# A retention layer and a top-1 mixture of experts in one launch: engine orders written by hand, compact states, and gathers that follow the scatters

## The chip, the core and the metric

The kernel runs on one core of one Trainium2 chip. The core has a matrix engine (PE; its weight loads are listed as PEld), a vector engine (DVE), a scalar engine (ACT), a general engine (POOL) and a queue engine (SP) that only starts transfers. PE reads from on-chip memory (SBUF) and writes to the accumulator memory (PSUM), which DVE and ACT empty. Transfers from and to HBM run on 16 DMA engines that all queues share. The metric is the device time of one execution in microseconds (us), as the median of several.

## The reference, cut to what matters

First a retention layer (decay gamma per head, state of 64x64 per head) over 4 batches, 8 heads and 768 positions; its output, 3072 rows of 512, goes into a mixture of experts with 8 experts, where a row is computed only if its skip score is positive, and then by the one expert with the largest logit.

```python
for t in range(S):                       # S = 768, D = 64, H = 8, B = 4
    state = gamma[None, :, None, None] * state + einsum('bhd,bhe->bhde', k[:, :, t], v[:, :, t])
    y[:, :, t] = scale * einsum('bhd,bhde->bhe', q[:, :, t], state)
x = y.transpose(0, 2, 1, 3).reshape(B * S, H * D)      # 3072 x 512
do_compute = (x @ w_skip) > 0
logits = x[do_compute] @ w_gate                          # 8 experts
e_idx = argmax(logits);  gate_w = softmax(logits)[e_idx]
out = x.copy()
out[rows of expert e] += gate_w * (relu(x @ w1[e]) @ w2[e])   # 512 -> 1024 -> 512
```

With the inputs of this case 1510 of the 3072 rows are computed; the experts get 191, 133, 229, 179, 211, 187, 160 and 220 of them.

## The kernel before, in words

**Stage 1, retention.** The recurrence is cut into 6 chunks of 128 positions per head, and two heads (a pair) are one unit: 4 batches x 4 pairs = 16 units. The decay is put into q and k beforehand (`scale_qk`, L85, on POOL: one instruction for k, one for q, in all units). A unit i then consists of these steps, most of them on PE in fp32, where a matmul becomes two instructions and a transpose one:

- `t_qk` (L198): 12 transposes of 128x128 in four groups of three; ACT copies each group from PSUM (L206) into KT and QT.
- `s_at` (L208), in two halves: k times q inside a chunk, as 64x64 tile matmuls (64 rows, 64 columns of the array), 24 instructions a half. DVE multiplies the two PSUM tiles of a half with the causal mask (L224) into ATm.
- `s_kv` (L230): 40 instructions of 64x64 tiles for k times v; DVE adds them up to running states Zb (L250, L252), in 10 instructions, one per chunk and head, each 64x64. Zb holds the two heads' states as blocks on the diagonal of a 128x128 tile whose other blocks are zero (L131 to L134).
- `s_inter` (L254), for unit i-1: 10 instructions, state times q, with the whole 128x128 array.
- `s_av` (L264), for unit i-1: 48 instructions of 64x64 tiles, ATm times v, into the same PSUM tiles Y; ACT copies them to xT (L276).
- `t_x` (L280), for unit i-2: 6 transposes back to rows; ACT copies them (L288) into xall, and after a batch's last pair xall is stored to the output tensor (L293).

After each batch come the gate's steps: `gate_logits` (L299), `gate_rows` (L311: logits, maximum, one-hot choice, softmax, running places per expert), and `slot_table` (L374), which gathers for every expert a table of up to 256 row numbers and gate weights by matmuls with one-hot matrices.

**Stage 2, experts.** `slots` (L435) makes row indices `si` from the table; empty slots get an index out of bounds, whose rows a transfer skips. `gather` (L453) fetches an expert's 256 rows from the output tensor with two indirect transfers on POOL. Then for each expert: `x_tr` (L462: DVE cast, 4+4 transposes, DVE copies), `layer1` (L474: 32 matmuls, relu on ACT), `layer2` (L490: 2 x 16 matmuls; DVE scales and adds, L499, into one of four buffers yo; POOL scatters, L502). PE's order is x_tr(e+1) ahead of layer2(e). The scatters are declared independent of each other, since their rows are distinct; gathers and scatters are not, so they are ordered on the output tensor.

**What sets the order.** A planner orders the instructions of PE, DVE, ACT and SP from priorities and its own estimates; POOL's order is as written (L69) up to the end of the gathers (L516). On POOL all 16 gathers (L513) and the late weight loads (L515) are written ahead of the first scatter. Expert weights (1 MB as bf16 each, 16 of them, cast on the way from fp32) are loaded by POOL's queue: eight are issued in stage 1 (`wunits`, L393), one right after it, seven between the gathers. q, k and v come by SP's queue, three units ahead (L398), 384 KB each.

Of the kernel before, what the change touches and what calls it, by code (L numbers as in the profile page):

```python
# [9 lines left out]
FP32 = mybir.dt.float32  # L10
# [8 lines left out]
def kernel(  # L19
# [36 lines left out]
    NEARLY = 5  # L56
    BIG = 1.0e6
# [10 lines left out]
    stP = ExitStack()  # L68
    stP.enter_context(tc.manual_schedule(engines={mybir.EngineType.Pool}))  # L69
# [15 lines left out]
    def scale_qk(i):  # L85
# [5 lines left out]
        for w, t, tag in ((kw, tk, "ks"), (qw, tq, "qs")):  # L91
# [3 lines left out]
            G_.tensor_tensor(o[:, :, :, :], in_, sc, ALU.mult)  # L95
            w[i] = o

    load(0)

# [11 lines left out]
    A_.activation(out=tq[:, :, :], in_=nlg[:, :, :], func=AF.Exp, bias=0.0, scale=1.0)  # L111
    V_.tensor_scalar(tq[:, :, :], tq[:, :, :], scale, None, ALU.mult)  # L112

    ident = poolC.tile([128, 128], FP32, name="ident")
    make_identity(nc, ident[:, :])

    load(1)
    scale_qk(0)


    maskc = poolC.tile([128, 4, R, 64], FP32, name="maskc")
    for r in range(R):
        for rq in range(R):
            for hi in range(2):
                V_.memset(maskc[64 * hi : 64 * hi + 64, r, rq, :], 1.0)
                G_.affine_select(
                    out=maskc[64 * hi : 64 * hi + 64, r, rq, :], in_=maskc[64 * hi : 64 * hi + 64, r, rq, :],
                    pattern=[[R, 64]], base=rq - r, channel_multiplier=-R, compare_op=ALU.is_ge, fill=0.0,
                )
    V_.tensor_copy(maskc[:, R : 2 * R, :, :], maskc[:, 0:R, :, :])  # L130
    Zb = [[poolC.tile([128, 128], FP32, name=f"Zb{s}_{c}") for c in range(1, NCH)] for s in range(2)]  # L131
    for zs in Zb:
        for z in zs:
            V_.memset(z[:, :], 0.0)  # L134
    load(2)

    identb = poolC.tile([128, 128], BF16, name="identb")
    V_.tensor_copy(identb[:, :], ident[:, :])
    ut_f = poolC.tile([128, 128], FP32, name="ut_f")
    make_upper_triangular(nc, ut_f[:, :], val=1.0, diag=False)  # L140
    utb = poolC.tile([128, 128], BF16, name="utb")
    V_.tensor_copy(utb[:, :], ut_f[:, :])
    onesb = poolC.tile([128, 128], BF16, name="onesb")
    V_.memset(onesb[:, :], 1.0)
    iota_i = poolC.tile([128, CAP], I32, name="iota_i")
    G_.iota(iota_i[:, :], pattern=[[1, CAP]], base=0, channel_multiplier=0)
    iotab = poolC.tile([128, CAP], BF16, name="iotab")
    V_.tensor_copy(iotab[:, :], iota_i[:, :])

# [434 lines left out]
```

## Time and profile before

| what | value |
|---|---|
| median of 3 runs | 260.09 us (256.2 to 260.12) |
| the profiled execution's own time | 257.54 us |
| its span, first to last instruction | 255.6 us |
| mean granted PE clock | 0.932 |
| PE busy | 204.7 us (80%) |
| DVE / ACT / POOL busy | 122.4 / 83.8 / 96.2 us |
| moved by DMA | 48.68 MB, mean 190 GB/s |

A busy PE is not PE at its peak: matmuls overlap, and what counts is the time from the start of one group to the start of the next. In the timeline's rows the columns are start, duration, engine, line and operation, output<-input, shape, number of instructions, and in brackets the idle time before the group with what ended it. Rows of the windows view give the stretch, its length, busy time (and instructions) of PE, PEld, DVE, ACT and POOL, the granted PE clock, the DMA engines' mean share and GB/s.

### The profile page before, as it was taken

The numbers are of one execution on the slowest core, as the hardware profiler recorded it, in microseconds if no ns is written. First come the engines' busy times: TensorE is split into PE (matmuls) and PEld (weight loads), VectorE is DVE, ScalarE is ACT, GpSimd is POOL, SyncE is SP. The second block draws the span as 40 slices with busy tenths as digits, with TensorE's granted clock in tenths as the row PEclk, the third lists the DMA queues.
The fourth block names the chain that finished last, engine by engine and source line by source line (L and its number), as shares of the span: only waits on it lengthen the run. The fifth ranks groups of instructions, "written<-read, shape, count | busy, mean of one in ns | idle before, by whom it ended". The sixth has DMA issues, their size and how long they took to land. (4 is left out here: it accounts for less than half of the span.)

```text
span 255.6 us, 7627 instructions
## 1 busy us (share of the span) xinstructions
PE 204.7 (80%) x3261; PEld 159.2 (62%) x3261; DVE 122.4 (48%) x432; ACT 83.8 (33%) x175; POOL 96.2 (38%) x102
## 2 busy tenths in 40 slices
PE   0889999998899978899998984189999308999900
PEld 0678889887678768677797753076658203566600
DVE  7376665538926646926638806324343103442210
ACT  2325544461544431544451540032224300123300
POOL 3875445414504531505610000787443064512220
PEclk9999999999999999999999997579999955999995
DMA  7998996999896999495999915389999992211120
GB/s 200 267 292 202 226 265 176 188 312 318 202 211 178 336 226 275 104 204 142 166 329 213 199 36 217 102 148 257 241 255 252 245 222 96 100 39 50 51 78 0
DMA packets 48261, 48.68 MB, mean 190 GB/s; under 512 B 3188, under 2 KB 40052, under 8 KB 47200
## 3 DMA queue, kind: packets, MB, share of 16 engines
q0 software_dynamic: 7936, 22.97, 41.4%
q1 hardware_dynamic: 38688, 18.90, 28.2%
q10 hardware_dynamic: 1600, 6.29, 6.4%
q8 instruction: 27, 0.44, 0.7%
q14 instruction: 10, 0.08, 0.1%
HBM read 56.64 MB, written 10.49 MB: 263 GB/s over the span
## 5 line engine op out<-in xcount | busy, mean ns | idle before, releaser
L224 DVE TENSOR_TENSOR ATm<-atps,maskc 128x384 f32<-128x384 f32 x64 | 32.7, 553 | 44.2 <-PE atps L219 43.7
L95 POOL TENSOR_TENSOR ks<-kw,tk 128x768 f32<-128x768 f32 x16 | 23.9, 1492 | 70.5 <-issue 43.7
L494 PE MATMUL yps<-w2b,hT 128*128 128x512 bf16 x128 | 31.7, 406 | 11.5 <-DVE yo L499 11.5
L485 ACT ACTIVATE hT<-hps 128x512 bf16<-128x512 f32 x32 | 19.0, 597 | 65.9 <-PE hps L481 65.9
L219 PE MATMUL atps<-QT,KT 64*64 64x128 f32 x768 | 32.1, 279 | 2.7 <-DVE ATm L224 2.6
L270 PE MATMUL yps<-ATm,vn 64*64 64x128 f32 x768 | 29.4, 272 | 2.8 <-issue 2.8
L481 PE MATMUL hps<-xgT,w1b 128*128 128x256 bf16 x256 | 30.6, 278 | 0.4 <-DVE xgT L472 0.2
L252 DVE TENSOR_TENSOR Zb<-kvps,Zb 64x64 f32<-64x64 f32 x128 | 28.4, 222 | 3.9
L494 PEld LDWEIGHTS <-hT 128*128 128x128 bf16 x128 | 13.0, 103 | 27.3 <-issue 15.6
L502 POOL DMA_INDIRECT out_dram<-yo,si x16 | 16.3, 1016 | 35.0 <-DVE yo L499 21.1
L481 PEld LDWEIGHTS <-w1b 128*128 128x128 bf16 x256 | 25.5, 100 | 5.6 <-issue 1.0
L219 PEld LDWEIGHTS atps<-QT,KT 64*64 64x64 f32 x768 | 23.7, 135 | 7.6 <-DVE ATm L224 4.3
L276 ACT COPY xT<-yps 128x384 f32<-128x384 f32 x32 | 13.9, 482 | 37.0 <-PE yps L270 37.0
L259 PE MATMUL yps<-QT,Zb 128*128 128x128 f32 x160 | 25.3, 276 | 0.8 <-DVE hm L334 0.8
L270 PEld LDWEIGHTS yps<-ATm,vn 64*64 64x64 f32 x768 | 23.1, 133 | 4.5 <-issue 4.5
L499 DVE SCALAR_TENSOR_TENSOR yo<-yps,g,xg 128x512 f32<-128x512 f32 x16 | 11.7, 748 | 26.4 <-PE yps L494 15.6
L95 POOL TENSOR_TENSOR qs<-qw,tq 128x768 f32<-128x768 f32 x16 | 23.9, 1494 | 0.2 <-DVE tq L112 0.2
L205 PE MATMUL tps<-ident,ks 128*128 128x128 f32 x96 | 17.5, 293 | 7.2 <-POOL ks L95 6.7
L206 ACT COPY KT<-tps 128x384 f32<-128x384 f32 x32 | 15.4, 480 | 22.5 <-PE tps L205 22.1
L456 POOL DMA_INDIRECT xg<-out_dram,si x16 | 18.0, 1125 | 11.7 <-DMA w1b<-in_moe_w_dram 4.2
L259 PEld LDWEIGHTS yps<-QT,Zb 128*128 128x128 f32 x160 | 21.3, 191 | 0.8 <-issue 0.8
L466 DVE CAST xb<-xg 128x512 bf16<-128x512 f32 x16 | 9.8, 624 | 22.4 <-DMA xg<-out_dram,si 22.4
(100 smaller groups left out, 235.3 us busy)
## 6 DMA issues: line engine op xcount, KB each, us to landing
w1b<-in_moe_w_dram POOLq DMA_DIRECT2D x8, 1024.0 KB, 11.0
w2b<-in_moe_w_dram POOLq DMA_DIRECT2D x8, 1024.0 KB, 13.8
kw<-in_k_dram SPq DMA_DIRECT2D x16, 384.0 KB, 4.9
qw<-in_q_dram SPq DMA_DIRECT2D x16, 384.0 KB, 6.2
vn<-in_v_dram SPq DMA_DIRECT2D x16, 384.0 KB, 6.7
out_dram<-xall ACTq DMA_DIRECT2D x4, 1536.0 KB, 9.9
xg<-out_dram,si POOLq DMA_INDIRECT x16, 11.0
out_dram<-yo,si POOLq DMA_INDIRECT x16, 2.7
```

Of the source, the lines that this page charges most:

```text
L95: G_.tensor_tensor(o[:, :, :, :], in_, sc, ALU.mult)
L205: PE.transpose(out=ps[:, j * 128 : (j + 1) * 128], in_=in_, identity=ident[:, :])
L219: PE.matmul(out=ps[h][cp, j * C : (j + 1) * C], lhsT=KT[i][hp, s_, cp], rhs=QT[i][hp, R * g : R * g + R, cp], start=True, stop=True,)
L224: V_.tensor_tensor(out=ATm[i, a][:, h, :, :], in0=ps[h][:, :].rearrange("p (c t) -> p c t", c=HB), in1=maskc[:, a : a + HB, :, :].rearrang ...
L252: V_.tensor_tensor(z, kv, Zb[i % 2][c - 1][hp, hp], ALU.add)
L259: PE.matmul(out=Y[i, c][:, g, :], lhsT=Zb[i % 2][ch - 1][:, :], rhs=QT[i][:, R * g : R * g + R, 64 * c : 64 * c + 64], start=(ch <= 2), st ...
L270: PE.matmul(out=Y[i, c][64 * h : 64 * h + 64, g, :], lhsT=vn[i][cp, h * G + g, r * D : (r + 1) * D], rhs=ATm[i, (R * g + r) // HB][cp, h, ...
L456: G_.indirect_dma_start(out=t[:, :], out_offset=None, in_=out[:, :], in_offset=bass.IndirectOffsetOnAxis(ap=si[:, st, e : e + 1], axis=0), ...
L481: PE.matmul(out=ps[:, f, :], lhsT=w1b[e][:, db, f2 * 256 + f : (f2 + 1) * 256 : 2], rhs=xgT[e][:, db, :], start=(db == 0), stop=(db == NDB ...
L485: A_.activation(out=hT[:, 2 * f2 : 2 * f2 + 2, :], in_=ps[:, :, :], func=AF.Relu, bias=0.0, scale=1.0)
L494: PE.matmul(out=ps[:, :], lhsT=hT[:, fb, st * 128 : (st + 1) * 128], rhs=w2b[e][:, fb, :], start=(fb == 0), stop=(fb == NFB - 1),)
L502: sc = G_.indirect_dma_start(out=out[:, :], out_offset=bass.IndirectOffsetOnAxis(ap=si[:, st, e : e + 1], axis=0), in_=yo[:, :], in_offset ...
```

## The change

- **Orders.** PE, DVE, ACT, POOL and SP all run as written in stage 1; PE, DVE and ACT also in stage 2. A unit's PE order is now: 12 transposes, 6 transposes back of unit i-2, the gate's step if any, `s_inter(i-1)`, `s_at(i,0)`, `s_kv(i)`, `s_av(i-1)`, `s_at(i,1)`.
- **PSUM.** The shared tag T has 4 buffers in place of 2, and `s_kv`'s tiles take theirs from it.
- **Compact states.** Zb is 128x64, the two heads one above the other; 5 DVE instructions a unit make it. `s_inter` is 10 matmuls (20 instructions) of 64x64 tiles; its two heads use different rows and columns of the array and write different partitions of one PSUM tile.
- **Start.** Masks by 4 instructions in place of 8, q of unit 0 scaled on DVE, loads of unit 1 moved up, other constants moved to unit 1.
- **Gate.** One step per unit after a batch (rows, places, table), 6 transposes and a DVE sum in place of 12 matmuls; the softmax after the places. For the last batch three pairs' logits are made ahead, the last pair's from xT directly, and the row numbers' table ahead of the gate weights'.
- **Last pair.** It is stored apart (three transfers of 128 columns), the other three pairs of that batch earlier.
- **Experts.** The indices of the gathers are clamped to the last row instead of being out of bounds, so that all 256 rows of an expert are fetched. xg has 4 buffers per half. Gathers 0 to 2, each with one weight, come first; after expert e's scatters come up to two weight loads and then gather e+3. Four experts' weights are loaded in stage 1, and eight loads are left for stage 2.

```diff
-    stP.enter_context(tc.manual_schedule(engines={mybir.EngineType.Pool}))
+    stM.enter_context(tc.manual_schedule(engines={ET.PE, ET.DVE, ET.Activation, ET.Pool, ET.SP}))
...
-        return psum.tile([128, HW], FP32, tag="T", bufs=2, name=name)
+        return psum.tile([128, HW], FP32, tag="T", bufs=4, name=name)
...
         for c in range(NCH - 1):
+            z = Zb[i % 2][c][:, :]
+            kv = ps[c % 2][:, (c // 2) * D : (c // 2 + 1) * D]
+            if c == 0:
+                V_.tensor_copy(z, kv)
+            else:
+                V_.tensor_tensor(z, kv, Zb[i % 2][c - 1][:, :], ALU.add)
+
+    def s_inter(i, chunks):
+        for ch in chunks:
+            g, c = divmod(ch, 2)
+            if g == 1 - c:
+                Y[i, c] = psum.tile([128, G, C], FP32, tag=f"Y{c}", bufs=1, name="yps")
             for h in range(2):
                 hp = slice(64 * h, 64 * h + 64)
+                PE.matmul(
+                    out=Y[i, c][hp, g, :], lhsT=Zb[i % 2][ch - 1][hp, :], rhs=QT[i][hp, R * g : R * g + R, 64 * c : 64 * c + 64],
+                    start=(ch <= 2), stop=False, skip_group_check=True,
+                )
...
+    for i in range(NU):
+        scale_qk(i + 1)
+        if i == 1:
+            more_constants()
+        if i in wunits:
+            load_w(*wjobs.pop(0), poolW)
+        load(i + 3)
+        b, p = divmod(i - 2, NP)
+        t_qk(i, kw, KT, "KT", 2, 0)
+        t_qk(i, qw, QT, "QT", 2, 0)
+        t_qk(i, kw, KT, "KT", 2, 1)
+        t_qk(i, qw, QT, "QT", 2, 1)
+        if i >= 2:
+            t_x(i - 2, 0)
+            t_x(i - 2, 1)
+        if i >= 6 and p == 0:
+            L = gate_rows(range(NP))
+        if i >= 6 and p == 1:
+            cp = places(b - 1, routed[1])
+        if i >= 6 and p == 2:
+            slot_table(psum, b - 1, oh, ALLV, "T", 4)
+        if i >= 1:
+            s_inter(i - 1, range(1, NCH))
+        s_at(i, 0)
+        s_kv(i)
+        if i >= 1:
+            s_av(i - 1)
+        s_at(i, 1)
+        if i >= 2 and p == NP - 1:
+            gate_logits(b, range(NP))
...
+    t_x(z - 1, 0)
+    s_inter(z, [1, 2])
+    gate_logits(B - 1, range(NP - 1))
+    t_x(z - 1, 1)
+    slot_table(psum, B - 2, oh, ALLV, "T", 4)
+    s_inter(z, range(3, NCH))
+    L = gate_rows(range(NP - 1))
+    s_av(z)
+    t_x(z, 0)
+    gate_last(z, L)
+    t_x(z, 1)
+    Ls, ha = route(L)
+    cp = places(B - 1, ha)
+    put_rhs(B - 1, ha, IDS)
+    put_places(B - 1, ha, cp)
+    oh = one_hots(pool, B - 1)
+    slot_table(psum, B - 1, oh, IDS, "T", 4)
...
+    for e in range(3):
+        gather(e, sg)
+        load_w(*late.pop(0))
...
     for e in range(E):
         hT = layer1(e)
         if e + 1 < E:
             x_tr(e + 1)
         layer2(e, hT, si, g, first=True)
+        with tc.issue_after(scatters[-1].ins):
+            for _ in range(2):
+                if late:
+                    load_w(*late.pop(0))
+            if e + 3 < E:
+                gather(e + 3, sg)
```

More of the change, by code (lines that the diff above doesn't have):

```diff
@@ L130 @@
+    scale_qk(0, (G_, V_))
     V_.tensor_copy(maskc[:, R : 2 * R, :, :], maskc[:, 0:R, :, :])
[L131 to L134, printed above, removed]
     load(2)
[L137 to L140, printed above, removed]
@@ L163 @@
[L163 to L168 removed]
+    Zb = [[poolC.tile([128, D], FP32, name=f"Zb{s}_{c}") for c in range(1, NCH)] for s in range(2)]
     Wc = poolC.tile([128, NDB, 32], FP32, name="Wc")
@@ L230, in s_kv @@
     def s_kv(i):
-        ps = [psum.tile([128, G * D], FP32, tag=f"KV{c}", bufs=1, name="kvps") for c in range(2)]
+        ps = [psum.tile([128, G * D], FP32, tag="T", bufs=4, name="kvps") for c in range(2)]
         for g in range(G):
```

386 lines of the change are left out of this document (197 added, 189 removed).

## The prediction

> **What bounds the kernel now.** I read the windows first, cut at the events that divide the work: start, units 2 to 15, their tail, the last gate, the experts' start, a gap, the rest of the experts, the end.
>
> ```profile
> span 255.6 us, 7627 instructions
> ...
> PEclk9999999999999999999999997579999955999995
> ```
>
> ```profile
> 0.00:21.48 21.48, 13.18 (x258) 11.10 (x258) 14.38 (x65) 5.94 (x13) 14.48 (x29) 1.00 1.06 255
> 21.48:145.82 124.34, 116.92 (x2429) 98.34 (x2426) 74.89 (x280) 54.95 (x122) 42.31 (x34) 1.00 0.92 224
> 145.82:149.57 3.75, 3.75 (x79) 3.34 (x76) 1.17 (x3) 0.96 (x2) 0.00 (x0) 1.00 0.16 33
> 149.57:160.45 10.88, 5.62 (x55) 3.62 (x54) 5.15 (x36) 2.92 (x7) 0.15 (x2) 0.79 0.37 146
> 160.45:200.30 39.85, 33.24 (x255) 24.00 (x256) 14.96 (x31) 11.26 (x19) 23.05 (x23) 0.89 0.95 214
> 200.30:211.57 11.27, 0.17 (x4) 0.05 (x1) 0.80 (x2) 0.60 (x1) 4.00 (x4) 0.65 0.93 230
> 211.57:245.43 33.86, 31.81 (x193) 18.75 (x192) 11.03 (x18) 7.17 (x12) 12.26 (x12) 0.91 0.18 68
> 245.43:255.60 10.17, 0.00 (x0) 0.00 (x0) 0.00 (x0) 0.00 (x0) 0.00 (x0) 0.63 0.07 22
> ```
>
> Half the span is the stretch of 14 units, where PE is busy 116.92 of 124.34 us, but the DMA engines' share is 0.92 as well: two resources stand near their limit. The experts take 84.98 us (160.45 to 245.43), and 11.27 of them are a hole in which PE does nothing while DMA works.
>
> The timeline shows what a unit costs on PE. This is unit 2, which has no gate step:
>
> ```profile
> 21.48 0.55 PE L205 MATMUL tps<-ident,ks 128*128 128x128 f32 x3
> 21.87 0.49 PE L205 MATMUL tps<-ident,qs 128*128 128x128 f32 x3
> ...
> 24.16 0.83 PE L259 MATMUL yps<-QT,Zb 128*128 128x128 f32 x6
> 24.83 0.49 PE L287 MATMUL tps<-ident,xT 128*128 128x128 f32 x3
> 25.25 0.89 PE L219 MATMUL atps<-QT,KT 64*64 64x128 f32 x24
> 25.95 0.81 PE L240 MATMUL kvps<-vn,ks 64*64 64x64 f32 x38
> ...
> 26.65 1.49 PE L270 MATMUL yps<-ATm,vn 64*64 64x128 f32 x46
> 27.91 0.88 PE L219 MATMUL atps<-QT,KT 64*64 64x128 f32 x24
> 28.72 0.55 PE L205 MATMUL tps<-ident,ks 128*128 128x128 f32 x3
> ```
>
> From start to start: three transposes 0.39 us (0.13 each); six of s_inter 0.67 (0.11 each); 24 of s_at 0.70, and 0.81 where transposes follow, so a change from tiles to the whole array costs about 0.1; s_kv with its last two 0.70; s_av 1.26. A unit takes 28.72 - 21.48 = 7.24 us. Fourteen of them would be 101.4 of the 124.34 us; the other 22.9 go to three batches' gates, 7.6 us each.
>
> The last gate and the experts:
>
> ```profile
> 149.61 0.86 ACT L276 COPY xT<-yps 128x384 f32<-128x384 f32 x2 [0.99 <-PE yps L270]
> ...
> 151.64 1.50 PE L304 MATMUL gps<-xT,Wc 128*32 128x384 f32 x16 [0.24 <-ACT xall L288]
> ...
> 153.09 1.51 PE L315 MATMUL lps<-sel,Gs 128*128 128x9 f32 x12
> ...
> 154.63 0.21 DVE L321 COPY L<-lps 128x54 f32<-128x54 f32 x1 [7.54 <-PE lps L315]
> ...
> 157.97 1.40 PE L384 MATMUL tabps<-rhsT,oh 128*128 128x40 bf16 x12 [1.24 <-DVE rhsT L363]
> ...
> 160.45 1.09 POOL L456 DMA_INDIRECT xg<-out_dram,si  x1 [1.02 <-DVE thr L534]
> ...
> 163.92 0.61 DVE L466 CAST xb<-xg 128x512 bf16<-128x512 f32 x1 [3.13 <-DMA xg<-out_dram,si]
> ```
>
> ```profile
> 192.11 1.26 POOL L456 DMA_INDIRECT xg<-out_dram,si  x1 [2.74 <-DMA w1b<-in_moe_w_dram]
> ...
> 206.06 1.04 POOL L502 DMA_INDIRECT out_dram<-yo,si  x1 [11.88 <-DMA xg<-out_dram,si]
> ...
> 211.57 6.47 PE L494 MATMUL yps<-w2b,hT 128*128 128x512 bf16 x16 [11.11 <-DVE yo L499]
> ...
> 217.94 3.62 PE L494 MATMUL yps<-w2b,hT 128*128 128x512 bf16 x16
> ...
> 221.39 3.69 PE L481 MATMUL hps<-xgT,w1b 128*128 128x256 bf16 x32
> ...
> 228.81 3.69 PE L481 MATMUL hps<-xgT,w1b 128*128 128x256 bf16 x32
> ...
> 244.45 0.98 POOL L502 DMA_INDIRECT out_dram<-yo,si  x1 [0.75 <-DVEq L543]
> ```
>
> Undisturbed, an expert takes PE 7.42 us (221.39 to 228.81). The hole is a wait for order on the output tensor: the first scatter had its data long before, stood behind the last gather (issued 192.11) on POOL, and waited 11.88 us more until that gather landed. All four yo stayed full, and layer2 stood. Sixteen matmuls after the hole took 6.47 us against 3.62: the granted clock had fallen (0.65 in the gap's row).
>
> The price of transfers, from three stretches of the DMA view: weights alone (138 to 144 us), q, k and v alone (12 to 21), both (27 to 30, two queues' lines).
>
> ```profile
> DMA packets 461, 1.33 MB, mean 222 GB/s; under 512 B 18, under 2 KB 18, under 8 KB 393
> ```
>
> ```profile
> DMA packets 4976, 2.51 MB, mean 279 GB/s; under 512 B 124, under 2 KB 4974, under 8 KB 4974
> ```
>
> ```profile
> q0 software_dynamic: 76, 0.61, 97.6%
> q1 hardware_dynamic: 78, 0.04, 6.5%
> ```
>
> A weight (1.05 MB) takes 4.7 us, a unit's q, k and v (1.18 MB) 4.2 us, and while a weight runs, q1 gets 0.04 MB of the 0.65 moved in 3 us: the two add up rather than overlap.
>
> **The change, part by part.**
>
> *Start.* Unit 2 begins at 21.48. Fewer masks and memsets, and q of unit 0 on DVE, bring unit 0 forward by 1 to 2.5 us. Against that the constants moved to unit 1 put some 14 DVE instructions (the copies waiting for POOL, which comes to them only after scaling unit 2's k and q) ahead of unit 1's mask multiplies; s_at's second half and unit 2 stand behind that. I take 22 us, ends 19 and 24.
>
> *The 14 units.* On PE: 18 transposes x 0.13 = 2.3; s_at 1.5; s_kv 0.7; s_av 1.3; switches 0.1 each way. s_inter becomes 20 tile instructions. No row shows two row tiles of the array writing one PSUM tile. s_at (rows differ, tiles differ) goes at 0.70/24 = 0.029 us an instruction, s_av (rows of a pair alike, one tile) at 1.26/46 = 0.027; I take 0.028, so 0.56 in place of 10 x 0.11 = 1.1. The other end is that the two heads take turns, below. Sum 6.5 us. Gates: logits 1.5, six transposes 0.8 in place of 1.51, places and table about 0.6: 2.9 a batch, in place of 7.6, because each step now has a unit's work behind it. PE needs 14 x 6.5 + 3 x 2.9 = 100 us. DVE has less to do than the 74.89 us of now (five state instructions a unit fewer), ACT gives one copy a unit away, POOL's 42.31 stay: none is late next.
>
> DMA is. Now it has 0.92 x 124.34 = 114 us of work there. One weight fewer is loaded in stage 1, and the last two may land after the stretch: 114 - 3 x 4.7 = 100 us. So two resources need 100 us each, with q1 starved whenever a weight runs; they can't both be met fully. I take 106, ends 100 and 118.
>
> *Tail.* The 3.75 us of PE get three quarters of the logits (1.1) and six transposes (0.8) more: 5.6. From there to the first gather, now 10.88: from the last s_av to L it was 5.06 (149.57 to 154.63); two xT copies side by side, three transposes, 12 matmuls on xT directly (as L315, 1.5) and one add make 2.9. L to table, 3.34, loses the softmax between: 3.1. Table to gather, 2.48, loses three DVE instructions: 2.3. Together 8.3. The stored last pair is 0.4 MB instead of 1.6 and is not late.
>
> *Experts.* From the first gather on (0), by the rows above: a gather's half lands 3.4 us after its issue (160.45 to 163.92), each further POOL transfer adds about 1.3. DMA then serves in order: gather 0 lands at 5; weight, gather 1 (256 rows, 0.52 MB, some 2.1 us at 222 to 279 GB/s) at 11.6; weight, gather 2 at 19; a third weight until 23.6. Scatter 0 is ordered behind gathers 0 to 2, so it starts at 19 and, with that weight ahead, lands at 25.5. Then the new wait: gather 3 reads the output tensor that scatter 0 wrote, so it is issued after that landing, and on POOL stands behind two weights: 9.4 us more of queue. It lands at 36.5; x_tr(3) stands in PE's order ahead of layer2(2), ready at about 27, and DVE's casts stand ahead of yo(2). Scatter 1 is in turn ordered behind gather 3. So the cycle scatter, landing, gather, landing is 2.6 + about 4 + 9.4 + 2.6 - overlap = 16 us with two weights, 11.3 with one, 9.3 with none (two scatters 2.6, landing 2.7 by the page's DMA line, two gathers 1.4 + 3.4 less the issue already counted), always above PE's 7.42:
>
> ```profile
> out_dram<-yo,si POOLq DMA_INDIRECT x16, 2.7
> ```
>
> Gathers 4 to 7 land at 52.5, 64, 73, 82.5. From the last: 1.6 for casts and transposes, layer2(6), 7.42 for expert 7, 2 for yo and scatter, part of it at a lower clock: end at 97, where it is 85 now. The hole of 11.27 goes, and several waits of 2 to 10 us take its place: +12.
>
> *Sum.* 22 + 106 + 5.6 + 8.3 + 97 + 10.2 (the end, unchanged) = 249.1 us of span. The profiled execution was 257.54 for 255.6 of span; with those 1.9 the sum is 251.0. The median of the runs (256.2 to 260.12) is 260.09, 1.0% above that execution; by the same ratio I forecast 254 us, own range 247 to 262.
>
> **The rivals.**
>
> *The gathers do not wait for the scatters* (or only for those of their own buffer). For it: nothing but that scatters are declared independent of each other. Against it: the 11.88 us wait above is just such an order, by landing and not by queue. Then DMA's order alone sets the experts, some 83 us: 14 less, 240.
>
> *The two heads of s_inter take turns.* Nothing in this trace shows it. If each of the 20 instructions takes as long as one of the whole array (0.11), 2.2 us a unit; midway 1.6, which is 1.0 more than in the forecast, 14 us over the stretch, of which the forecast's 6 us above PE's need cover some: +9, 263.
>
> [...] No row before shows the case, and the chance stays low because the two heads write different partitions.
>
> *DMA, not PE, sets the stretch, and it comes out slower.* Weights at units 2, 4, 6 and on each hold q1 up for 4.7 us; with PE faster, the loads have less time ahead, and the in-order engines stand for every late one. If the stretch keeps 120 us while the experts still lose 12: 249.1 + 14 = 263, that is 268. For it: the share of 0.92 now, and the two lines of 27 to 30 us. Against: loads are three units ahead, and unit 2 ran at 7.24 with the same loads. It decides from 117 us on.
>
> **How the numbers follow.** Forecast 0.52; gathers free 0.16; heads in turns 0.12; DMA-bound 0.13; 0.07 for what I don't see, on either side. A measurement of this kernel can't tell less than about 2%, here 5.2 us: faster is below 254.9, slower above 265.3. The forecast's own range lies half below 254.9: 0.26, with 0.16 and 0.04 of the unseen that is 0.46. Slower: 0.11 of DMA-bound, 0.03 of heads in turns, 0.04: 0.18. Within 2%: 0.36. The range 239 to 266 holds the forecast, most of the heads' case and half of the free gathers; left out are half of 0.16, most of 0.13.
>
> **What would show it.** Right: one run of tile matmuls a unit, unit starts 6.5 to 7.5 apart, gate batches without 7 us of extra; POOL's gathers 3 to 7 waiting for DMA of scatters, scatters for DMA of gathers, PE idle ahead of x_tr(3) and x_tr(4) by about 10 us; first gather near 142. Wrong: gathers 3 to 7 issued right behind the scatters without a wait; s_inter above 0.8 us a unit; POOL's scaling waiting for kw or qw in the middle units; an experts' stretch below 88 us.

## The result: slower, and the profile after

The changed kernel takes 276.25 us (median of 4 runs, 274.33 to 278.18) where the kernel before takes 260.11 on the same chip: a ratio of 1.072, interval 1.054 to 1.090. Slower, where 254 us were forecast. Some executions of a kernel are 1.5% or more above its fastest; the ratios here and below leave these out, the medians don't. The profiled execution took 278.18 us, its span 276.5 us. The page of the kernel after, its head and the row of the granted clock:

```profile
span 276.5 us, 7896 instructions
...
PE 206.4 (75%) x3417; PEld 163.8 (59%) x3417; DVE 114.3 (41%) x355; ACT 74.8 (27%) x175; POOL 92.9 (34%) x97
...
PEclk9999999979979979799999955999658589979985
...
q8 instruction: 29, 0.48, 0.7%
```

The windows of the kernel after, cut at the same events as before: start, units 2 to 15, tail, last gate, then the experts (four cuts at PE's two longest pauses), the end. Columns: stretch, length, busy time of PE, PEld, DVE, ACT and POOL, granted clock, DMA share, GB/s.

```profile
0.00:19.76 19.76, 12.67 (x269) 11.27 (x269) 11.08 (x42) 5.89 (x14) 11.06 (x24) 1.00 1.01 250
19.76:145.25 125.49, 111.98 (x2550) 100.82 (x2547) 62.20 (x202) 46.10 (x121) 43.14 (x34) 0.95 0.87 219
145.25:153.56 8.31, 7.45 (x104) 4.71 (x104) 5.58 (x24) 1.99 (x6) 0.00 (x0) 1.00 0.35 127
153.56:161.20 7.64, 3.78 (x37) 3.07 (x37) 4.70 (x24) 1.68 (x4) 0.00 (x0) 0.81 0.24 71
161.20:190.65 29.45, 21.57 (x165) 14.96 (x165) 11.58 (x32) 6.57 (x11) 14.04 (x15) 0.82 0.92 198
190.65:200.19 9.54, 0.00 (x0) 0.00 (x1) 0.64 (x2) 0.60 (x1) 0.12 (x1) 0.77 0.86 201
200.19:210.72 10.53, 10.49 (x56) 5.93 (x56) 2.94 (x5) 1.79 (x3) 5.52 (x6) 0.72 0.69 132
210.72:217.91 7.19, 0.00 (x0) 0.00 (x1) 0.65 (x2) 0.60 (x1) 0.00 (x0) 0.65 0.85 211
217.91:266.21 48.30, 38.48 (x240) 23.02 (x240) 14.91 (x25) 9.55 (x16) 19.00 (x19) 0.91 0.36 101
266.21:276.50 10.29, 0.00 (x0) 0.00 (x0) 0.00 (x0) 0.00 (x0) 0.00 (x0) 0.56 0.07 24
```

| stretch | before | forecast | after |
|---|---|---|---|
| start | 21.48 | 22 | 19.76 |
| units 2 to 15 | 124.34 | 106 | 125.49 |
| tail | 3.75 | 5.6 | 8.31 |
| last gate to first gather | 10.88 | 8.3 | 7.64 |
| experts | 84.98 | 97 | 105.01 |
| end | 10.17 | 10.2 | 10.29 |

Two things happened: the experts became 20 us longer, and the units, which were to give 18 us back, gave nothing.

**The experts.** The timeline of the kernel after, POOL and DVE in the middle of the experts; in brackets the idle time ahead and what ended it:

```profile
200.90 1.02 POOL L584 DMA_INDIRECT out_dram<-yo,si  x1 [10.13 <-DVE xb L550]
...
203.21 0.85 POOL L192 DMA_DIRECT2D w2b<-in_moe_w_dram  x1
204.01 0.63 POOL L189 DMA_DIRECT2D w1b<-in_moe_w_dram  x1
205.00 1.06 POOL L541 DMA_INDIRECT xg<-out_dram,sg  x1 [0.35 <-issue]
...
218.62 1.02 POOL L584 DMA_INDIRECT out_dram<-yo,si  x1 [11.24 <-DVE xb L550]
...
223.41 1.05 POOL L541 DMA_INDIRECT xg<-out_dram,sg  x1 [1.62 <-DMA out_dram<-yo,si]
...
236.80 1.03 POOL L541 DMA_INDIRECT xg<-out_dram,sg  x1 [3.33 <-DMA out_dram<-yo,si]
...
243.04 1.03 POOL L584 DMA_INDIRECT out_dram<-yo,si  x1 [3.89 <-DVE xb L550]
...
247.80 1.03 POOL L541 DMA_INDIRECT xg<-out_dram,sg  x1 [2.43 <-DMA out_dram<-yo,si]
...
253.43 1.03 POOL L584 DMA_INDIRECT out_dram<-yo,si  x1 [3.27 <-DVE xb L550]
```

```profile
199.52 1.26 DVE L550 CAST xb<-xg 128x512 bf16<-128x512 f32 x2 [11.58 <-DMA xg<-out_dram,sg]
217.24 1.26 DVE L550 CAST xb<-xg 128x512 bf16<-128x512 f32 x2 [9.23 <-DMA xg<-out_dram,sg]
...
252.69 0.61 DVE L550 CAST xb<-xg 128x512 bf16<-128x512 f32 x1 [0.80 <-DMA xg<-out_dram,sg]
```

Read one turn: gather 3 lands (199.52), scatter 1 goes (200.90), two weights are put on the queue, gather 4 is issued at 205.00 and lands 12.2 us later, behind the weights (217.24), and only then scatter 2 goes (218.62). That is the mutual wait of the prediction, gather for scatter and scatter for gather. (The scatters' rows name the cast xb, DVE's copy of the gathered rows to bf16, which ends about 0.1 us before each and itself waited for the gather.) PE stands for it twice, for 9.54 and 7.19 us, and the 16 matmuls behind each pause take 5.99 and 5.67 us where an undisturbed group takes 3.62: the clock is at half from 195.78 to 206.02 and from 212.85 to 223.09 us.

**The units.** An undisturbed unit is a little shorter than before, 6.67 us (19.76 to 26.43) against 7.24. What PE waited for in the stretch, from the waits view of the kernel after, and the same view of the kernel before:

```profile
PE atps L221 <- issue: 3.4, 3, 1.8
PE tabps L437 <- DVE oh L428: 3.0, 2, 1.5
PE tps L207 <- issue: 2.7, 1, 2.7
PE yps L275 <- issue: 2.6, 1, 2.6
PE yps L261 <- issue: 1.4, 1, 1.4
```

```profile
PE yps L270 <- issue: 2.8, 2, 2.3
...
PE lps L315 <- issue: 0.9, 1, 0.9
```

"issue" is time in which PE waited for nothing that the profile shows. It is 10.1 us now, 3.7 before. And behind some of the pauses the granted clock is down, which it never was in this stretch before. One of the two waits for the one-hots, in the timeline and in windows of 2 us of the kernel after:

```profile
75.35 1.39 PE L437 MATMUL tabps<-rhsT,oh 128*128 128x40 bf16 x12 [1.50 <-DVE oh L428]
76.67 2.19 PE L261 MATMUL yps<-QT,Zb 64*64 64x128 f32 x18
```

```profile
76.00:78.00 2.00, 1.99 (x21) 1.75 (x23) 0.97 (x4) 0.00 (x0) 0.00 (x0) 0.58 1.07 198
78.00:80.00 2.00, 2.00 (x43) 2.00 (x42) 0.00 (x0) 0.16 (x1) 0.00 (x0) 0.57 1.13 217
80.00:82.00 2.00, 2.00 (x94) 2.00 (x92) 1.72 (x6) 0.00 (x0) 1.03 (x1) 1.00 0.97 186
```

The clock falls to half for 3.41 us at a time, four times in the stretch (from 55.84, 76.31, 100.21 and 113.86 us), twice behind a pause for issue and twice behind one for the one-hots. 17 instructions of s_inter take 1.76 us there from start to start (114.88 to 116.64) for 0.94 at full clock (84.81 to 85.75), so half of the time at half clock is taken as lost: an estimate of 4 x 3.41 / 2 = 6.8 us. The four start 20.47, 23.90 and 13.65 us apart, which is 6, 7 and 4 times 3.41, and the two stretches above in the experts, of 10.24 us each, are 3 times as long. A pause of 1.50 us was followed by one here, while the pause of 2.35 us in the kernel before was not.

### The profile page after: what moved, and what is told of

Read it like the earlier page. It is cut to its first block, busy times and chain, and to the rows that moved or that the text cites. A ratio compares the mean times of both kernels' runs of the same rounds, so it can differ in the third digit from the quotient of the medians.

```text
span 276.5 us, 7896 instructions
## 1 busy us (share of the span) xinstructions
PE 206.4 (75%) x3417; PEld 163.8 (59%) x3417; DVE 114.3 (41%) x355; ACT 74.8 (27%) x175; POOL 92.9 (34%) x97
## 5 line engine op out<-in xcount | busy, mean ns | idle before, releaser
L221 PE MATMUL atps<-QT,KT 64*64 64x128 f32 x768 | 36.2, 287 | 3.4 <-issue 3.4
L576 PE MATMUL yps<-w2b,hT 128*128 128x512 bf16 x128 | 35.0, 436 | 0.0
L541 POOL DMA_INDIRECT xg<-out_dram,sg x16 | 16.9, 1057 | 43.9 <-DVE Rsum L412 30.9
L221 PEld LDWEIGHTS atps<-QT,KT 64*64 64x64 f32 x768 | 28.1, 141 | 4.5 <-issue 4.2
L275 PE MATMUL yps<-ATm,vn 64*64 64x128 f32 x768 | 28.0, 272 | 3.6 <-issue 3.6
L556 PE MATMUL xtp<-identb,xb 128*128 128x128 bf16 x64 | 7.4, 253 | 30.1 <-DVE xb L550 30.0
L261 PE MATMUL yps<-QT,Zb 64*64 64x128 f32 x320 | 23.7, 293 | 1.4 <-issue 1.4
L556 PEld LDWEIGHTS <-xb 128*128 128x128 bf16 x64 | 4.4, 110 | 33.3 <-DVE xb L550 33.3
L95 POOL TENSOR_TENSOR qs<-qw,tq 128x768 f32<-128x768 f32 x15 | 22.4, 1494 | 0.7 <-DMA qw<-in_q_dram 0.7
L261 PEld LDWEIGHTS yps<-QT,Zb 64*64 64x64 f32 x320 | 19.0, 144 | 3.7 <-issue 3.5
```

Of the source, the lines that this page charges most:

```text
L95: eng.tensor_tensor(o[:, :, :, :], in_, sc, ALU.mult)
L221: PE.matmul(out=ps[h][cp, j * C : (j + 1) * C], lhsT=KT[i][hp, s_, cp], rhs=QT[i][hp, R * g : R * g + R, cp], start=True, stop=True,)
L261: PE.matmul(out=Y[i, c][hp, g, :], lhsT=Zb[i % 2][ch - 1][hp, :], rhs=QT[i][hp, R * g : R * g + R, 64 * c : 64 * c + 64], start=(ch <= 2), ...
L275: PE.matmul(out=Y[i, c][64 * h : 64 * h + 64, g, :], lhsT=vn[i][cp, h * G + g, r * D : (r + 1) * D], rhs=ATm[i, (R * g + r) // HB][cp, h, ...
L541: G_.indirect_dma_start(out=xg[e, st][:, :], out_offset=None, in_=out[:, :], in_offset=bass.IndirectOffsetOnAxis(ap=sg[:, st, e : e + 1], ...
L576: PE.matmul(out=ps[:, :], lhsT=hT[:, fb, st * 128 : (st + 1) * 128], rhs=w2b[e][:, fb, :], start=(fb == 0), stop=(fb == NFB - 1),)
```

## The experiments

Each is compared with the kernel before on the same chip; "first gather" and "last scatter" are the starts of these on POOL in one execution, the profiled one, of `after` 161.2 and 265.2, of `before` 160.45 and 244.45.

### a1: all gathers first

```diff
-    for e in range(3):
+    for e in range(E):
         gather(e, sg)
+    for _ in range(3):
         load_w(*late.pop(0))
...
-            if e + 3 < E:
-                gather(e + 3, sg)
```

> The changed kernel with all eight experts' gathers written ahead of the first scatter (eight buffers per half in place of four); the weight loads stay where they are, three first and up to two after each expert's scatters. Theory (each gather 3 to 7 waits for the landing of a scatter and each scatter for a gather, with two weights queued between): the experts' stretch, 105 us from first gather to last scatter, falls below 85, since DMA serves gathers in about 18 us and the weights then come in time; time about 276 - 22 = 254 us. Rival (the order of the transfers by bytes alone sets the stretch, the mutual wait is only where it shows): the stretch stays above 97, time above 268.

Measured: 256.02 us, ratio 0.979 (0.961 to 0.998). First gather 159.9, last scatter 244.3. The windows of a1, units and experts:

```profile
19.36:144.00 124.64, 110.44 (x2550) 99.07 (x2547) 62.20 (x204) 45.65 (x120) 41.96 (x33) 0.96 0.89 221
...
159.90:245.24 85.34, 67.09 (x461) 43.11 (x461) 29.22 (x64) 19.00 (x32) 38.83 (x40) 0.90 0.77 182
```

The experts are back at 85 us, just above what was expected; beside the order, only the buffers for four more experts' rows differ, and the first three weight loads, which follow all gathers. So the order of gathers and scatters cost 20 us, more than the whole loss, and everything else in the change together is worth 2%, between 0.2 and 4. The units stayed at 125 us.

### a2, c1, d1, d2: what the loads of stage 1 do to the units

Four kernels of which only stage 1 is read. a2 loads no weight there. The others add, to a2, 1 MB of loads in each of units 5 to 14 into a tile that nothing reads: c1 by SyncE's queue, d1 by GpSimd's software queue, d2 by the same with a change to bf16.

```diff
-    wunits = (2, 4, 6, 8, 10, 12, 14, 15)
+    wunits = ()
...
+        if 5 <= i < NU - 1:
+            idle = poolQ.tile([128, 2, F], FP32, tag="idle", bufs=2, name="idle")
+            nc.sync.dma_start(out=idle[:, :, :], in_=moe_w1[i % E].rearrange("(p a) f -> p a f", p=128)[:, 0:2, :])
```

In d1 and d2 `G_.dma_start` stands in place of `nc.sync.dma_start`, in d2 `BF16` in place of `FP32`; the second edit isn't in a2.

> The changed kernel with no expert weight loaded in stage 1: all 16 loads follow the first gathers, so the experts' stretch becomes much longer and only stage 1 is read. Theory (PE's pauses in mid-sequence, 1.4 to 2.7 us each, are its instructions coming late because their fetch stands behind a weight on the DMA engines): the pauses that wait for nothing shown, 11 us in all, fall below 4, the clock stays at 1.00 up to the gate's own waits, and the first gather comes at 161 - 12 = about 149 us or earlier. Rival (the pauses come from the faster instruction stream itself or from q, k and v): five pauses or more remain and the first gather stays above 156.

> As a2_no_stage1_weights (no weight is loaded in the first stage), and besides SyncE's queue loads 1 MB of expert weights in each of units 5 to 14 into a tile that nothing reads. Only the first stage is read; the weights come late as in a2. Theory (TensorE's pauses that wait for nothing shown are instructions that come late when the DMA engines are full, whoever fills them): between 54 and 135 us, where a2 has no such pause, there are at least three of 1 to 3 us, each ending 1 to 2 us behind a 16 KB packet of the instruction queue, the clock behind them falls below 1, and the first gather comes 4 to 12 us after the 149.8 us of a2. Rival (the pauses belong to the weights' own software queue, which casts): none of them, first gather within 2 us of 149.8.

> As c1_useless_loads, with the useless 1 MB of each of units 5 to 14 started by GpSimd, on its software queue, still from fp32 to fp32. Only the first stage is read. Theory (the pauses come with GpSimd's software queue, whatever it moves): at least three pauses of 1 to 3 us that wait for nothing between 54 and 135 us, the clock behind them below 1, first gather 4 to 12 us after the 149.8 us of a2_no_stage1_weights. Rival (it is the change of type): as c1, first gather within 2 us of 150.7.

> As d1_useless_pool_queue, with the useless loads changed from fp32 to bf16 on the way, as a weight is. Only the first stage is read. Theory (software queue as such): as d1 within 2 us. Rival (the change of type makes the transfers small, 0.04 of 0.65 MB in 3 us for the other queues): first gather 4 to 12 us after 149.8 us here and not in d1.

The windows of a2, c1, d1 and d2, from the start of unit 5, where the useless loads begin, to 140 us, in this order, a block for each:

```profile
42.80:140.00 97.20, 91.31 (x2080) 80.09 (x2078) 56.04 (x194) 38.31 (x101) 26.74 (x19) 0.98 0.51 157
```

```profile
40.20:140.00 99.80, 91.40 (x2066) 79.65 (x2065) 55.90 (x193) 38.31 (x101) 27.75 (x19) 0.98 0.78 257
```

```profile
41.20:140.00 98.80, 88.97 (x2025) 79.73 (x2025) 50.99 (x172) 36.67 (x96) 33.23 (x29) 0.95 0.78 256
```

```profile
42.90:140.00 97.10, 88.56 (x1956) 79.57 (x1958) 49.52 (x166) 36.37 (x95) 33.23 (x29) 0.93 0.81 207
```

| kernel | from unit 5 to first gather | waits for issue in it | at half clock, half of it lost | more than a2 |
|---|---|---|---|---|
| a2, no loads | 42.8 to 149.8: 107.0 | 1.7 | 3.4: 1.7 | |
| c1, SyncE | 40.2 to 150.7: 110.5 | 4.4 | 3.4: 1.7 | 3.5 |
| d1, GpSimd | 41.2 to 156.2: 115.0 | 6.6 | 10.2: 5.1 | 8.0 |
| d2, GpSimd, bf16 | 42.9 to 158.1: 115.2 | 5.3 | 13.7: 6.8 | 8.2 |
| after, its own weights | 43.9 to 161.2: 117.3 | 7.1 | 13.7: 6.8 | 10.3 |

(The waits and the clock are read up to 140 us.) What the two columns of loss have above a2's gives the last one within 0.8 us in each row: what the loads cost the units is pauses for issue and time at half clock, and little else. Not all of the clock stands behind pauses for issue: of the stretches at half clock, one in a2, c1 and d1 and two in d2 and after follow a wait for the one-hots, which all five have.

Without weights the first gather comes 11.4 us earlier, as expected of a2; its waits for issue, 4.6 us where under 4 were expected, all lie before 54 us. The clock didn't stay at 1.00, as it should have, but was at half once, behind the one-hots. Useless traffic on the hardware queue brings two pauses of over 1 us behind 54 us, where three were expected; by the first gather alone, 0.9 us, its rival seemed right, but unit 5 began 2.6 us earlier than in a2 by less pausing ahead of any difference between the two. From the software queue the same bytes cost twice as much (with two pauses behind 54 us, where three were expected again), and the change of type adds nothing that can be told. So neither the weights' use nor the cast is needed for the pauses; traffic is enough. That the software queue is worse as such rests on single executions, and 3.4 of its 4.5 us are clock, which one pause more or less decides.

What runs ahead of a pause's end can be seen. This is the DMA view of the kernel after, from 97.9 to 99.2 us, inside the pause of 97.53 to 100.15:

```profile
q0 software_dynamic: 32, 0.21, 79.1%
...
q8 instruction: 1, 0.02, 4.6%
```

One packet of 16 KB of the instruction queue runs there, beside a weight on q0. In the traces of all kernels here, every pause of over 0.7 us in the units whose row says "issue" ended 2.2 to 2.8 us after the start of such a packet (in the kernel after 2.29, 2.72, 2.37, 2.20 and 2.36 us, in the kernel before 2.44 and 2.29). The places of the pauses have something in common too. Count all records of PE in the trace, matmuls, weight loads and its sequencer's, up to a pause: in the kernel after the five of 1.4 us and more stand behind 961, 1218, 1986, 3778 and 5314 of them, in the kernel before the two of over 0.7 us behind 3522 and 5058. Each of these is a multiple of 256 plus 193 or 194, and so it was for all 82 pauses of over 0.7 us for issue between 19 and 150 us that were counted in the 17 traces here. The number of packets is near that of such multiples: 29 in all on the queue in the kernel after, where 2 x 3417 instructions of PE are 26.7 times 256. The pauses cost 10 us there. That PE stood because its instructions came late is a reading of these agreements; no run changed how the instructions come, and why PE pauses at one of the multiples and not at the next stays open.

### a3: weights in pieces

```diff
-        if i in wunits:
-            load_w(*wjobs.pop(0), poolW)
+        npc = 0 if i < 2 else 1 if i < 14 else 2
+        for _ in range(npc):
+            load_piece(*pieces.pop(0))
```

(The same loop again behind `more_constants()`; a piece is 256 KB of bf16.)

> The changed kernel with each of the eight weights of stage 1 loaded in four pieces of 256 KB, spread over units 2 to 15. Theory (a whole weight fills the DMA queues for 4.7 us, and fetches of instructions and loads of q, k, v stand behind it): with 1.2 us at a time the pauses shrink; first gather at 150 to 156 us, time 266 to 271. Rival (only the total of bytes matters): first gather within 2 us of 161, time 274 to 278.

Measured: 281.5 us, ratio 1.081 (1.063 to 1.099), first gather 162.6; waits for issue no shorter than in the kernel after, one of them 4.30 us. Not the length of a queue of one weight, then: spreading it out made nothing better.

### a4: the order of s_inter

The ten matmuls in the order (1,0) (2,1) (3,0) (4,1) (5,0) (2,0) (1,1) (4,0) (3,1) (5,1), chunk and head:

```diff
-        for ch in chunks:
+        for ch, h in order:
...
-            for h in range(2):
+            for h in (h,):
```

> The changed kernel with the ten matmuls of s_inter reordered so that neighbours differ in the head and in the PSUM tile they write. In the changed kernel 17 of its 20 instructions take 0.93 us, 0.055 each. Theory (two row tiles of the array that write the same PSUM tile take turns): 20 instructions take 0.55 to 0.65 us, a unit 6.3 instead of 6.67, the whole 2 to 5 us less. Rival (a pair on the diagonal of the array takes 0.05 whatever it writes): unchanged within 0.1 us a unit.

Measured: 276.87 us, ratio 1.065 (1.053 to 1.077), like the changed kernel. The timeline of the kernel after and of a4, the bulk of one s_inter:

```profile
21.87 1.19 PE L261 MATMUL yps<-QT,Zb 64*64 64x128 f32 x17
22.80 0.32 PE L221 MATMUL atps<-QT,KT 64*64 64x128 f32 x1
```

```profile
20.63 1.19 PE L265 MATMUL yps<-QT,Zb 64*64 64x128 f32 x17
```

17 instructions from start to start in 0.93 us: 0.055 each, 1.1 us for the 20, as much as the ten whole-array instructions took. s_at and s_av go at 0.029 and 0.027. If two row tiles took turns because they write the same PSUM tile, a4, where neighbours write different ones, would have run faster; it didn't. What makes these pairs slow stays open.

### b1, b3, b2, c4, c2: the parts of stage 1, from a1 on

b1 moves the slot table behind s_av. The other edits start from a1 (b3), b3 (b2) and b1 (c4, c2).

```diff
-        if i >= 6 and p == 2:
-            slot_table(psum, b - 1, oh, ALLV, "T", 4)
         if i >= 1:
             s_inter(i - 1, range(1, NCH))
...
             s_av(i - 1)
+        if i >= 6 and p == 2:
+            slot_table(psum, b - 1, oh, ALLV, "T", 4)
```

> The changed kernel with all sixteen gathers first (as in a1_gathers_first) and, besides, the slot table of a batch moved from the beginning of its unit to a place behind s_av and ahead of s_at(i, 1). Theory (part of the lost time of the 15 units is TensorE standing at the head of the slot table for one-hots that VectorE makes after the gate weights, 1.50 and 1.51 us, and the slower clock behind each): those two pauses go, the clock of their units is 1.0, and the first gather comes 3 to 6 us earlier than the 159.9 us of a1_gathers_first; time 250 to 253. Rival (the units are paced by the DMA engines, which are busy 0.87 of the stretch, and a pause taken out is given back at the next load): the pauses go and the first gather still comes within 1.5 us of 159.9.

Measured: 252.05 us, ratio 0.965 (0.951 to 0.979), first gather 155.7. The waits view of b1's units holds no one-hots any more:

```profile
PE atps L221 <- issue: 5.4, 3, 2.4
PE yps L275 <- issue: 5.1, 3, 2.7
PE yps L261 <- issue: 0.6, 1, 0.6
```

The two waits are gone and the first gather comes 4.2 us earlier than in a1, as the theory had it: 3.0 of it is the waiting, 0.4 an earlier unit 2. Its part on the clock isn't borne out: the units are at half clock for 10.2 us in either kernel, and the waits for issue are the same 11 us. The ratios' intervals overlap, so the gain rests on the two profiled executions.

b3, whole states:

```diff
-    Zb = [[poolC.tile([128, D], FP32, name=f"Zb{s}_{c}") for c in range(1, NCH)] for s in range(2)]
+    Zb = [[poolC.tile([128, 128], FP32, name=f"Zb{s}_{c}") for c in range(1, NCH)] for s in range(2)]
...
-                PE.matmul(
-                    out=Y[i, c][hp, g, :], lhsT=Zb[i % 2][ch - 1][hp, :], rhs=QT[i][hp, R * g : R * g + R, 64 * c : 64 * c + 64],
+            PE.matmul(
+                out=Y[i, c][:, g, :], lhsT=Zb[i % 2][ch - 1][:, :], rhs=QT[i][:, R * g : R * g + R, 64 * c : 64 * c + 64],
```

> The changed kernel with all gathers first and the compact states undone: the states of the two heads lie on the diagonal of a 128x128 tile again, five whole-array matmuls and ten VectorE additions of half a tile in each unit in place of ten 64x64 matmuls and five additions. Theory (ten 64x64 matmuls on the diagonal take about 0.05 us each, as the groups of 17 in 0.93 us show, and so 0.5 against 5 x 0.22 = 1.1 us of before at most; half of that hidden): first gather 0 to 4 us later than 159.9. If compact states are worth what the prediction summed, 0.56 us a unit, it is 8 us later; if nothing, within 1.5 us of it.

b2, the planner's order in stage 1:

```diff
-    stM.enter_context(tc.manual_schedule(engines={ET.PE, ET.DVE, ET.Activation, ET.Pool, ET.SP}))
+    stM.enter_context(tc.manual_schedule(engines={ET.Pool}))
```

> As b3_whole_states (the changed kernel with all gathers first and the states of two heads in one 128x128 tile), and besides the orders of TensorE, VectorE, ScalarE and SyncE in the units are left to the planner; only GpSimd's is by hand. Theory (the hand order of the engines is worth next to nothing, as TensorE's list under the planner differs from it only in that s_at(i, 1) starts among s_av): first gather within 3 us of that of b3_whole_states. Rival (the hand order gave what a1_gathers_first gained over the kernel before): first gather over 4 us later.

Measured: b3 ratio 0.970 (0.957 to 0.983), first gather 159.7; b2 ratio 0.977 (0.958 to 0.996), first gather 158.2; a1 had 0.979 and 159.9. The first gathers lie where the expectations had them for parts worth nothing or next to nothing, and the ratios can't be told apart: neither the compact states nor the engines' hand order is worth anything that can be measured. PE's waits for issue in the units are 6.1 us in b3 and 7.6 in b2, between the 3.7 of the kernel before and the 11.0 of a1. Why the kernel before stood so little under as much traffic stays open.

c4, the gate steps in one unit, the slot table in the next (for the batch before the last too, whose table stands in the tail otherwise):

```diff
         if i >= 6 and p == 0:
+            L = gate_rows(range(NP))
             routed = route(L)
-        if i >= 6 and p == 1:
+            cp = places(b - 1, routed[1])
             put_places(b - 1, routed[1], cp)
```

> As b1_table_later, with the gate steps of a batch no longer spread over units: rows, routing, places, one-hots stand together behind s_at(i, 1) of one unit, the slot table in the next. TensorE then stands at the places until VectorE has made the routing, some 4 to 6 us in each of three batches. Theory (the stretch of 14 units is paced by TensorE, its pauses and its clock): first gather 10 to 18 us later than 155.7. Rival (the stretch is paced by the DMA engines, which would catch up while TensorE stands): at most 5 us later.

Measured: 258.27 us, ratio 0.999 (0.992 to 1.005), first gather 159.1. From the waits view of c4:

```profile
PE cps L383 <- DVE ha L373: 5.0, 3, 1.9
```

Three pauses of 1.6 us, not 4 to 6: that size was wrong. They cost 3.4 us up to the first gather, where the theory had 10 to 18 and the rival at most 5. The ratio's interval lies apart from b1's. The medians are 6 us apart, but on different chips; c2 below, on c4's chip and with b1's first gather, is 3 us faster than c4 by the medians, which is the cost to go by. Spreading the gate is the one part of stage 1 here that pays. Of the 5.0 us that PE stood, 3.4 came through to the first gather in these executions, so the catching up that the rival sees covers about a third of it.

c2, the last batch stored together:

```diff
-        if a == 0 or i < NU - 2 and p < NP - 1:
+        if a == 0 or p < NP - 1:
...
-            cs = slice(DM - 128, DM) if last else slice(0, DM - 128)
+            cs = slice(0, DM)
```

> As b1_table_later, with the storing of the last pair apart undone: the last batch's rows leave in three transfers of 512 KB behind the last pair's transposes instead of three of 384 KB before and three of 128 KB behind. Theory (ScalarE gives 1.7 us to the three early issues, and the late ones land 3.9 to 5 us after issue instead of 2.2; the row numbers that the first gather also needs are ready at 155.7): first gather 1 to 3 us later than the 155.7 of b1_table_later. If storing apart gives nothing: within 0.7 us of it.

Measured: 255.21 us, ratio 0.984 (0.974 to 0.995), first gather 155.7 as in b1. Storing the last pair apart gives the first gather nothing; the 3 us in the medians arise behind it, on different chips, and the two ratios' intervals overlap.

### b4, c3, d3: can it be better

b4 is b1 with the two weights of expert 4 loaded in the tail; c3 is b4 with other units for the weights; d3 is b1 with seven weights as fp32 halves on SyncE's queue and ScalarE making bf16 of them.

```diff
-    NEARLY = 4
+    NEARLY = 5
...
     z = NU - 1
+    load_w(*wjobs.pop(0), poolW)
     t_x(z - 1, 0)
...
     t_x(z, 1)
+    load_w(*wjobs.pop(0), poolW)
```

> As b1_table_later, and the two weights of expert 4 are loaded in the last part of the first stage (one ahead of the last unit's t_x, one behind its gate), where the DMA engines are busy 0.24 to 0.35 of the time, into room that the gathered rows leave by going to the second stage's pool. Theory (the experts' stretch of 85 us is paced by the weights that are still to be loaded, 8 of them of some 9 to 11 us of the queue each): the last scatter comes 6 to 14 us after less than in b1_table_later, time 240 to 247. Rival (the stores of the last pair, which the first gather waits for, share the engines with the two weights and land later by what is gained): first gather 4 to 8 us later and the time within 3 us of b1_table_later.

```diff
-    wunits = (2, 4, 6, 8, 10, 12, 14, 15)
+    wunits = (5, 6, 8, 9, 10, 12, 14, 15)
```

> As b4_tail_weights, with the eight weights of the units started in units 5, 6, 8, 9, 10, 12, 14, 15 instead of 2, 4, 6, 8, 10, 12, 14, 15. Theory (the pause near 34 us, 2.11 us with a slower clock behind it, comes of the first weight on top of the q, k and v loads): that pause is gone or under 1 us and unit 5 begins 2 to 4 us earlier than the 44.6 us of b4_tail_weights; the first gather 0 to 3 us earlier than 157.9. Rival (the pause only moves to where the weights now are): first gather within 1 us of 157.9 or later.

```diff
+        if 1 <= i < NU - 1:
+            load_half(*halves.pop(0))
         load(i + 3)
...
         s_kv(i)
+        if i >= 2:
+            to_bf16()
```

> As b1_table_later, with seven of the eight weights of the units loaded as fp32 halves of 1 MB by SyncE's queue, one half in each of units 1 to 14, and changed to bf16 by ScalarE a unit later, between s_kv and s_av (2 to 3 us each, where ScalarE is busy 0.37 of the time); the eighth goes as before in the last unit, the rest of the stage and the experts are unchanged, but that all gathered rows lie in the second stage's pool. Theory (software queue or its change of type slows the units): first gather 3 to 8 us earlier than the 155.7 of b1_table_later, time 244 to 249. Rival (a late half holds up ScalarE, and with it the PSUM buffers that TensorE needs, or the traffic itself costs): first gather at 155 or later, time not below 251.

Measured: b4 250.87 us, ratio 0.960 (0.946 to 0.974), the fastest here; its experts, in its windows:

```profile
157.90:239.60 81.70, 66.41 (x461) 43.70 (x461) 29.08 (x62) 19.10 (x32) 37.28 (x38) 0.89 0.67 165
```

81.7 us against 86.05 in b1, a gain of 4.4 where 6 to 14 were expected, and the first gather came 2.2 us later: in all too small a gain to tell from b1. c3: 251.58 us, ratio 0.969 (0.961 to 0.976), first gather 159.0; the pause near 34 us is still there (1.82) with no weight near it. Unit 5 began 3.3 us earlier, as the theory said, but that was lost again up to the first gather, so the rival holds. d3: 258.0 to 265.0 us beside 255.7 to 264.2 of the kernel before, no gain, first gather 161.1. Its waits view tells why the hardware queue didn't help:

```profile
PE yps L303 <- issue: 6.0, 3, 3.0
PE atps L249 <- issue: 3.9, 2, 2.3
PE yps L303 <- ACT touch L297: 3.2, 4, 1.6
PE tps L235 <- issue: 2.3, 1, 2.3
```

3.2 us for ScalarE, held up by 14 casts of 1.9 us, and 12.2 us of waits for issue in these rows, 11.1 in b1's: with weights on SyncE's queue the pauses are there too. What c1 and d1 seemed to say against the software queue is no rule, then. Which loads bring how much of the pauses stays open.

## Why the prediction was wrong

By its sum: start -2.2, units +19.5, tail +2.7, last gate -0.7, experts +8.0, end +0.1: +27.4 us of span.

*The 14 units: the step that failed.* The stretch took 125.49 us, outside its ends of 100 and 118. PE's need was nearly right. An undisturbed unit is 6.67 us for 6.5. A batch's gate adds, by the units of a2 without waits, 1.4 for the logits, about 0.9 for the rows, 0.4 for the places, and 1.5 for the table: 4.2 for 2.9, and two of the three tables lie in the stretch. 14 x 6.67 + 3 x 2.7 + 2 x 1.5 = 104, for 100. DMA's need was not: 0.87 x 125.49 = 109 us for 100. Eight weights started in the stretch and all eight landed there, the last at 142.7 us; the two that were to land later didn't, and the kernel before had only most of a ninth there. The addition of 6 us above the 100 of PE and DMA was to cover all that doesn't meet; 13.0 us of pauses (10.0 in five pauses for issue, 3.0 for one-hots) and 6.8 of clock came instead. "None is late next" was wrong for the one-hots, which DVE makes behind the gate weights while PE's list asks for them early in the next unit, ahead of its tile matmuls. The pauses for issue had no term at all. They were in the profile before, 2.35 us at 94.19, and went unread.

*s_inter.* 0.56 us a unit was forecast, 1.1 measured. The rival "in turns" had a price of 2.2 and a midway of 1.6; even that was too much, but its doubt was right; against the shared PSUM tile as the cause speaks a4. That is 14 x 0.5 = 7 us of expected gain that wasn't there, and b3 shows that the old form is no worse. The unit still came to 6.67 because its other parts are 0.4 us shorter than summed, which was luck.

*Tail and last gate.* The 8.31 us hold more PE work than forecast (7.45 busy for 5.6); the table of the batch before the last, which the sum had in the units, falls there. The gate's 7.64 were as summed, 0.7 better. Together they gained nothing: 15.95 for 14.63.

*Experts.* The mechanism was right, and a1 shows it by taking it away. Sizes short: from scatter to scatter 18.6 and 17.7 us with two weights (16 forecast), 12.5 with one (11.3), 11.9 and 10.4 with none (9.3). The last turn, by the rows shown: 4.76 us from scatter to gather, 4.89 until the gather's second half has landed, 0.74 to the next scatter; the last two were summed as 4. The five turns take 71.1 us, for the 63.5 from 19 to 82.5; the first scatter comes 2.1 later than said, and what follows the last gather is 1.7 shorter. That the chance of "slower" was still low is the sum's doing: 18 us of gain were set against 12 of loss, where the loss was sure and the gain was not.

*What was to show it.* Right: the waits of gathers 5 to 7 for scatters by name, PE's pauses ahead of x_tr(3) and x_tr(4) (9.54 and 7.19 us for 10), experts above 88 us, the end, and the start within its bounds (though unit 0 came forward by 0.6 us and not by 1 to 2.5). Wrong: unit starts 6.7 to 11.9 us apart where 6.5 to 7.5 was said, first gather at 161.2 for 142, s_inter above 0.8.

*The rivals.* Gathers that don't wait: refuted by POOL's rows. DMA-bound stretch: it gave 268 and came nearest, and the decisive 117 us were passed, but its mechanism, in-order engines standing for late loads, is hardly in the waits: POOL's scaling stood 5.0 us for q in the middle units, 4.3 before, and PE for no load; it stood 10.1 us for issue. What was right in it is that DMA had more to do than summed, and that traffic brings the pauses.

## What to carry to other kernels

A gather that reads the tensor a scatter writes must not be put behind that scatter if it doesn't need it: order on the whole tensor made each turn last a full round of both transfers and all that is queued between, and issuing all gathers first took 20 us away. When a stage is tightened, read first what its pauses are now, also those for which the profile names nothing: here they grew from 3.7 to 10.1 us, and a pause can cost its length again in clock (one of 1.50 us was followed by 3.41 us at half clock). A part that shortens PE's work counts only where PE's work is what ends last; of the four parts of the first stage that were undone here, one paid, and moving one table by a few lines (b1) gave about as much, by the first gathers.

## What was not expected of the hardware

- Pairs of 64x64 matmuls whose tiles differ in rows and columns took 0.055 us an instruction, in either order of writing, against 0.027 to 0.029 for those of s_at and s_av; the gain of the smaller tiles was nil.
- PE paused for 0.7 to 4.3 us, for nothing that the profile names, and went on 2.2 to 2.8 us after a 16 KB packet of the instruction queue began, in all 82 cases behind a multiple of 256 of its records plus 193 or 194; 10 us of the changed kernel's stage 1.
- A pause of 1.50 us was followed by 3.41 us at half clock in the kernel after, and one of 2.35 us in the kernel before by none.
